# Low parts of w_in on VectorE alone, and 65 columns of v a head, in a decay-attention and hard-swish MoE kernel

## The chip, the core and the metric

The kernel runs on one NeuronCore of a Trainium2 chip. The metric is the device time of one execution in microseconds (us). A core has TensorE (matmuls; PE in the profile, its weight loads PEld), VectorE (DVE), ScalarE (ACT), GpSimd (POOL) and SyncE (SP, which issues the transfers here). Each engine works off its own queue of instructions in order.

## The reference

```python
def _attn_ref(q, k, v, f):          # 8 batches, 8 heads, 576 rows, 64 columns
    scale = 1.0 / np.sqrt(D)
    scores = scale * np.matmul(q, k.transpose(0, 1, 3, 2))
    log_f = np.log(np.clip(f, 0.0001, 1.0))
    cum = np.cumsum(log_f, axis=-1)
    decay = cum[:, :, :, None] - cum[:, :, None, :]
    causal = np.triu(np.ones((S, S), dtype=bool), k=1)
    scores = np.where(causal, -1000000000.0, scores + decay)
    ...
    attn = attn / (np.sum(attn, axis=-1, keepdims=True) + 1e-09)
    return np.matmul(attn, v).astype(np.float32)

def _moe_ref(x, w_in, w_out):       # 4608 x 512, 512 x 2048, 2048 x 512
    h = x @ w_in
    relu6 = np.clip(h + 3.0, 0.0, 6.0)
    g = h * relu6 / 6.0
    return (g @ w_out).astype(np.float32)
```

`x` is the attention's result with the heads side by side. `w_in` and `w_out` come as 64-bit floats.

## The kernel before

Large matmuls run in 16-bit floats with split operands: a value is a high part (its f16 rounding, scaled by a power of two) plus a low part (the f16 rounding of what is left), and a product is three matmuls, high with high, high with low and low with high.

**Weights.** Each of w_in and w_out comes in 16 chunks of 512 KB. `w_load` fetches a chunk, `w_decode` rebuilds f32 values from the 64-bit words (one ScalarE instruction L251, two of VectorE L252 and L253) and squares them on ScalarE for a scale (L257). `w_split` then writes the high part on ScalarE (L284) and the low part in one of these ways:

- with `eye` (a diagonal matrix of minus the scale, L317 on VectorE): TensorE forms minus scale times x by an f32 matmul (L287), adds the high part by an f16 matmul with the identity (L288), and ScalarE copies minus the sum from PSUM to f16 (L289);
- otherwise one VectorE instruction, scale times x minus high (L295), or ScalarE and GpSimd where `POOL_REST` says so, which is nowhere here.

w_in has four groups of four chunks, each with a scale of its own; `PE_LOW` says which groups take the first way: (1, 1, 1, 0), so 12 chunks of 16. All of w_out takes L295. The f32 values of w_in lie in `gT`, those of w_out in `w2`, in the space that the tiles of the MoE take later.

**Attention.** The list `VH` sets the order of the work: four pairs of heads of batch 0 with their first 256 rows (kind A, VH numbers 0 to 3), the eight heads of batch 0 with the rows that are left (kind B, 4 to 11), and the 56 heads of the other batches (kind F). For A and B, `natural` forms scores for the row maxima (pn, L487, with the maximum on VectorE at L493), `max_rows` turns the maxima into a row (ptm, L502; mr, L504; a transfer to TQ), `scores` forms transposed scores (ps, L551 to L554) with exponentials on ScalarE (L570), and `av` multiplies them with v in f32 (L705). For F, `rows` forms the scores once (pn, L611 and L614), VectorE takes the maxima (pp, L622), ScalarE the exponentials (L634), and the two parts go through `ring` (L648 to L662) and a transposing transfer to f16 matmuls with v (L694 to L699).

The product with v ends in `pav`, one tile in PSUM with five blocks of `NAV` columns. A row of v holds 65 columns a head, 64 of v and one of ones for the row sum, 520 for the eight heads. The f32 product reads 96 columns from where its head begins, or for the last head the last 96 of the 520; `window` gives the first column and the head's offset in it. The division by the row sum (L726 to L732, VectorE) reads the 65 that count.

**MoE.** `h_unit` forms 128 columns of h (L777 to L779), its activation (L783, L786) and g's two parts (L787, L788) in `gT`; `out_unit` forms 128 rows of the output (po, L824 to L826, L830). Batch 0 is done in two halves of 256 rows.

**Order.** The program is written as one loop over `VH`. In each step the steps of the weights (`w_step`, by `W_RATE`) and of the MoE (`fill`, by a credit and `F_RATE`) are called between the pieces of the attention. A scheduler then sets each engine's order by its own estimates of durations and by that program order, so that an edit in one place moves instructions elsewhere.

Of the kernel before, what the change touches and what calls it, by code (L numbers as in the profile page):

```python
# [20 lines left out]
def kernel(  # L21
# [12 lines left out]
    NHEAD, D, S = qk.shape  # L34
    D //= 2
    B = vS.shape[0]
    H = NHEAD // B
# [52 lines left out]
    INIT_POOL = (1, 1, 1)  # L90
    W_FIRST = 2
    GRAM = (0, 0, 0, 0)
    PE_LOW = (1, 1, 1, 0)
    QA = 256
    CA = QA // P
    VH = [("A", g) for g in range(NPAIR)] + [("B", n) for n in range(H)]
# [24 lines left out]
        eng.memset(TK[i].bitcast(F32)[96:97, :], 1.0)  # L121
        eng.memset(TK[i].bitcast(F32)[:, S:], 0.0)

    NAV = 96
    pav = ps_a.tile([P, NCH, NAV], F32, name="pav")

    NV16 = 3
    v16 = cpool.tile([P, NV16, NCH, 2, VW + 1], F16, name="v16")
    VR = H * (D + 1)
# [18 lines left out]
    def v_chunk(b, c):  # L148
        return v_parts(b)[c // 3][:, c % 3]
# [51 lines left out]
    def scol(c):  # L201
        return SC[:, c:c + 1]
# [94 lines left out]
    def w_in_work():  # L297
# [6 lines left out]
        for j in range(NG):  # L304
# [9 lines left out]
            eye = None  # L314
            if PE_LOW[j]:
                eye = p2.tile([P, DM], F32, tag="o", name=f"eye{j}")[:, 0:P]
# [210 lines left out]
    def blocks(v):  # L527

        kind, n = VH[v]
        if kind == "A":  # L530
            return [
                (2 * n + h, c, h * CA + c, P,
                 [(j, h * (2 * QA - P) + (c * P if j == 0 else QA), P) for j in range(c + 1)])
                for h in range(2) for c in range(CA)
            ]
        nq = S - QA
        off = [0, nq, 2 * nq, 3 * nq, 3 * nq + nq - P]
        return [
            (n, c, c, CR[c],
             [(j, off[j] + (c - max(j, CA)) * P, CR[j]) for j in range(c + 1)])  # L540
            for c in range(CA, NCH)
        ]
# [43 lines left out]
    o = 0  # L586
# [86 lines left out]

    xpair = {}

    def window(head):

        o = head % H * (D + 1)
        w0 = min(o, VR - NAV)
        return w0, o - w0  # L680

    def av(v, ph):
        kind, n = VH[v]
        g = n if kind == "A" else n // 2
        b = g // NPAIR
        vt = v16[:, g % NV16]
        if kind == "F":
            jh = n % 2
            blk = [(n, c, c) for c in range(NCH)]
            vh, vl = vt[:, :, jh, 0:D + 1], vt[:, :, jh, D + 1:VW]  # L690
            for c in range(NCH):
                pb = ph[:, HT[c]:HT[c] + (2 * c + 1) * P].rearrange("p (g t) -> p g t", t=P)
                o1, o0 = pav[:, c, 0:D + 1], pav[:, c, 0:D]
                nc.tensor.matmul(o1, pb[:, c], vh[:, 0], start=True, stop=False)  # L694
                nc.tensor.matmul(o0, pb[:, c], vl[:, 0], start=False, stop=(c == 0))
                for k in range(1, c + 1):
                    nc.tensor.matmul(o1, pb[:, c + k], vh[:, k], start=False, stop=False)
                    nc.tensor.matmul(o0, pb[:, c + k], vl[:, k], start=False, stop=False)  # L698
                    nc.tensor.matmul(o1, pb[:, k - 1], vh[:, k], start=False, stop=(k == c))  # L699
        else:  # L700
            blk = blocks(v)
            for head, c, pl, m, js in blk:
                w0, _ = window(head)
                for jc, o, kk in js:
                    nc.tensor.matmul(  # L705
                        pav[:m, pl, :], ph[:kk, o:o + m], v_chunk(b, jc)[:kk, w0:w0 + NAV],
                        start=(jc == 0), stop=(jc == c),
                    )
        heads = sorted({x[0] for x in blk})
        if heads[0] % 2 == 0:  # L710
            xpair[g] = (
                p2.tile([P, NCH, P], F32, tag="xf", name=f"xf_{v}", bufs=1),
                p2.tile([P, NCH, 2, P], F16, tag="xhl", name=f"xhl_{v}", bufs=1),
            )
        xf, xhl = xpair[g]
        for head in heads:
            jh = head % 2
            mine = [x for x in blk if x[0] == head]
            p0, p1 = mine[0][2], mine[-1][2] + 1
            c0, c1 = mine[0][1], mine[-1][1] + 1  # L720
            vo = window(head)[1] if b == 0 else 0
            rs = p2.tile([P, NCH, 1], F32, tag="rs", name=f"rs_{v}_{jh}")[:, p0:p1]
            total = pav[:, p0:p1, vo + D:vo + D + 1]
            if b == 0:

                nc.vector.tensor_scalar(  # L726
                    rs, total, PSC * 1e-9, scol(IV + b), op0=ALU.add, op1=ALU.mult
                )
            else:
                nc.vector.tensor_scalar(rs, total, PSC * 1e-9, None, op0=ALU.add)  # L730
            nc.vector.reciprocal(rs, rs)
            nc.vector.tensor_tensor(  # L732
                xf[:, c0:c1, jh * D:(jh + 1) * D], pav[:, p0:p1, vo:vo + D],
                rs.to_broadcast([P, p1 - p0, D]), op=ALU.mult,
            )
        if heads[-1] % 2:
            nc.scalar.copy(xhl[:, c0:c1, 0], xf[:, c0:c1])
            nc.vector.tensor_tensor(
                xhl[:, c0:c1, 1], xf[:, c0:c1], xhl[:, c0:c1, 0], op=ALU.subtract
            )  # L740
# [218 lines left out]
    for i, (kind, n) in enumerate(VH):  # L959
        b, h = divmod(n, H)  # L960
        if kind == "A":
            b = h = 0
# [51 lines left out]
        if prev is not None:  # L1014
            av(*prev)
            if VH[prev[0]][0] == "A" or VH[prev[0]][1] % 2 == 1:
                pend_x = prev[0]
# [3 lines left out]
        prev = (i, ph)  # L1021
    rates[0] = 1.0
    av(*prev)
    fill(4)
    x_move(prev[0])
# [39 lines left out]
```

## Time and profile before

| | |
|---|---|
| median of 3 runs | 1072.47 us (1071.74 to 1077.68) |
| the profiled execution | 1069.33 us, its span 1067.5 us |
| mean granted TensorE clock | 0.988 |
| batch 0's twelve VH steps | roughly the first 135 us |
| first wide row maximum of batch 1 (L622, 576 columns) | starts at 135.2 us |
| first activation on VectorE (L786) of the second half of batch 0 | starts at 202.2 us |
| first activation on VectorE (L786) of batch 1 | starts at 259.9 us |

The profile is of one execution, taken by the hardware's profiler. Busy times are unions of an engine's instructions. Matmuls overlap and their ends are modelled, so the distance from start to start tells more of a matmul's cost than its length. A wait is put down to what came last. The chain that ended last is followed back from the last instruction, at each step to what released it, or to the instruction before it on its engine; "issue" in it is time for which the profile shows no wait.

### The profile page before, as it was taken

What the parts mean: (1) busy time and instruction counts of PE and PEld (TensorE: products, weight loads), DVE (VectorE), ACT (ScalarE), POOL (GpSimd) and SP (SyncE); (2) the same over time, 40 slices, a digit from 0 to 9 for tenths busy, and PEclk for the clock granted to TensorE, in tenths of its full rate; (3) what the DMA queues carried; (4) which work ended last, traced back from release to release, by engine and by line L of the source; (5) the groups of instructions that cost most, each with busy time, mean ns of one, the idle gap of its engine ahead of it and who ended that gap; (6) DMA issues with size and microseconds to landing.
All of it is one profiled execution on the core that took longest, in us unless ns stands there. A gap on an engine that the chain in (4) does not pass through costs nothing.

```text
span 1067.5 us, 21157 instructions
## 1 busy us (share of the span) xinstructions
PE 1006.3 (94%) x7650; PEld 598.0 (56%) x7650; DVE 731.1 (68%) x1887; ACT 587.3 (55%) x1189; POOL 403.4 (38%) x505
## 2 busy tenths in 40 slices
PE   2799977899999999999999999999999999999897
PEld 1577844665555755555555755555555755444543
DVE  6978899996876768866886668846895677105300
ACT  4778666764764557545654557635764566115301
POOL 8343466443443444344443444534443330000000
PEclk9989989999999999999999999999999999999999
DMA  8965647955856776667575766566557554010000
GB/s 240 308 187 194 151 109 145 220 114 118 169 116 134 139 153 124 113 148 165 118 134 118 158 140 119 118 136 167 119 112 145 103 100 74 12 40 1 1 20 30
DMA packets 259155, 133.78 MB, mean 125 GB/s; under 512 B 226948, under 2 KB 228540, under 8 KB 259052
## 3 DMA queue, kind: packets, MB, share of 16 engines
q1 hardware_dynamic: 259052, 132.44, 55.7%
q8 instruction: 60, 0.98, 0.4%
q14 instruction: 43, 0.35, 0.1%
HBM read 47.93 MB, written 9.73 MB: 54 GB/s over the span
## 4 chain that ended last, share of the span: by engine, by line
PE 76%; DVE 12%; ACT 5%; issue 4%; DMA 2%; POOL 1%; SPq 0%; DVEq 0%; ACTq 0%; POOLq 0%
PE po L824 9%; PE po L826 9%; PE po L825 9%; PE ph L777 9%; PE ph L778 9%; PE ph L779 9%; PE pn L611 3%; PE pn L614 3%; DVE pp L622 2%; DVE ring L651 2%; PE po_r L826 1%; PE pav L698 1%; ACT pp L634 1%; PE po_r L824 1%; PE po_r L825 1%
## 5 line engine op out<-in xcount | busy, mean ns | idle before, releaser
L634 ACT ACTIVATE pp<-pp,nb 128x192 f32<-128x192 f32 x280 | 138.6, 552 | 170.3 <-DVE nb L628 150.8
L777 PE MATMUL ph<-xT,w 128*128 128x512 f16 (+1 forms) x576 | 198.8, 357 | 2.5 <-DVE r L786 2.4
L825 PE MATMUL po<-w,gT 128*128 128x512 f16 x512 | 192.6, 382 | 8.0 <-DVE w L295 8.0
L779 PE MATMUL ph<-xT,w 128*128 128x512 f16 (+1 forms) x576 | 198.0, 356 | 0.0
L778 PE MATMUL ph<-xT,w 128*128 128x512 f16 (+1 forms) x576 | 197.8, 356 | 0.0
L651 DVE TENSOR_TENSOR ring<-pp,ring 128x128 f16<-128x128 f32 (+2 forms) x216 | 138.0, 650 | 85.6 <-ACT ring L648 84.7
L824 PE MATMUL po<-w,gT 128*128 128x512 f16 x512 | 190.4, 383 | 5.8 <-DVE r_r L813 2.7
L826 PE MATMUL po<-w,gT 128*128 128x512 f16 x512 | 192.4, 383 | 0.0
L622 DVE CUSTOM_DVE_ANT_0 pp<-pn,W 128x192 f32<-128x192 f32 x280 | 123.3, 482 | 29.3 <-PE pn L614 28.0
L461 POOL TENSOR_TENSOR T<-ST,T 64x576 fp32r<-64x576 f32 (+1 forms) x68 | 100.9, 1483 | 107.2 <-DMA T<-TK 85.8
L786 DVE SCALAR_TENSOR_TENSOR r<-r,ph 128x512 f32<-128x512 f32 (+1 forms) x144 | 89.1, 620 | 61.4 <-ACT r L783 60.6
L611 PE MATMUL pn<-TK,TQ 68*128 68x192 f32 x336 | 124.8, 385 | 3.8 <-issue 2.2
L788 DVE TENSOR_TENSOR gT<-r,gT 128x512 f16<-128x512 f32 (+1 forms) x144 | 111.6, 781 | 22.0 <-ACT gT L787 20.6
L614 PE MATMUL pn<-T,T 128*128 128x192 f32 x336 | 115.2, 368 | 0.2 <-POOL T L461 0.2
L783 ACT ACTIVATE r<-ph,bias_r,SC 128x512 f32<-128x512 f32 (+1 forms) x144 | 103.9, 725 | 19.2 <-PE ph L779 17.1
L648 ACT CAST ring<-pp 128x192 f16<-128x192 f32 x280 | 114.2, 449 | 0.0
L787 ACT CAST gT<-r 128x512 f16<-128x512 f32 (+1 forms) x144 | 81.4, 567 | 59.6 <-DVE r L786 59.3
L449 POOL TENSOR_SCALAR TK<-ST 64x576 fp32r<-64x576 f32 (+1 forms) x68 | 49.2, 724 | 167.8 <-PE pn L611 142.9
L657 POOL TENSOR_TENSOR ring<-pp,ring 128x128 f16<-128x128 f32 x96 | 61.0, 636 | 116.1 <-ACT ring L648 75.2
L458 POOL TENSOR_TENSOR T<-ST,TQ 64x576 fp32r<-64x576 f32 (+2 forms) x68 | 95.2, 1400 | 17.7 <-PE pn L614 11.1
L826 PEld LDWEIGHTS <-gT 128*128 128x128 f16 x560 | 54.8, 98 | 74.5 <-issue 15.1
L825 PEld LDWEIGHTS <-gT 128*128 128x128 f16 x560 | 54.9, 98 | 66.5 <-issue 11.9
(158 smaller groups left out, 2010.2 us busy)
## 6 DMA issues: line engine op xcount, KB each, us to landing
ST<-in_qk_dram SPq DMA_DIRECT2D x64, 288.0 KB
T<-TK SPq DMA_DIRECT2D x64, 144.0 KB
ring<-in_w_out_dram SPq DMA_DIRECT2D x16, 512.0 KB
out_dram<-o SPq DMA_DIRECT2D x32, 256.0 KB
T<-TQ SPq DMA_DIRECT2D x56, 144.0 KB
vst<-in_vS_dram SPq DMA_DIRECT2D x7, 1040.0 KB
ring<-in_w_in_dram SPq DMA_DIRECT2D x9, 512.0 KB
w<-in_w_in_dram SPq DMA_DIRECT2D x7, 512.0 KB
```

Source lines behind the costliest of these rows:

```text
L611: nc.tensor.matmul(dst, TQ[i][0:D + 4, qs], TK[i][0:D + 4, a:e], start=True, stop=False)
L614: nc.tensor.matmul(dst, T7[j][:, qs], T1[j][:, a:e], start=False, stop=True)
L622: nc.vector.tensor_tensor_reduce(pp[:r, w:w + kw], pn[:r, o:o + kw], W[:r, 4 * P + r - kw:4 * P + r], 1.0, -3.0e38, ALU.add, ALU.max, accu ...
L634: nc.scalar.activation(x_, x_, AF.Exp, bias=nb[:r, e0 + x:e0 + x + 1], scale=0.125)
L648: nc.scalar.copy(hl[:r, h0[c]:h0[c] + kw], pp[:r, at[c]:at[c] + kw])
L651: eng.tensor_tensor(hl[:r, a:a + c * P], pp[:r, at[c] + 64:at[c] + kw], hl[:r, h0[c] + 64:h0[c] + kw], op=ALU.subtract,)
L777: nc.tensor.matmul(ph, w1[0][:, cc, fs_], xh, start=(cc == 0), stop=False)
L778: nc.tensor.matmul(ph, w1[0][:, cc, fs_], xl, start=False, stop=False)
L779: nc.tensor.matmul(ph, w1[1][:, cc, fs_], xh, start=False, stop=(cc == NCC - 1))
L824: nc.tensor.matmul(po, g[:, 0, fc, ts_], w2[:, fc, 0, :], start=(fc == 0), stop=False)
L825: nc.tensor.matmul(po, g[:, 0, fc, ts_], w2[:, fc, 1, :], start=False, stop=False)
L826: nc.tensor.matmul(po, g[:, 1, fc, ts_], w2[:, fc, 0, :], start=False, stop=(fc == NFC - 1))
```

## The change

No group of w_in takes the way over TensorE and ScalarE any more: all 16 chunks have their low part made by L295 on VectorE. And the f32 product with v reads the 65 columns of its head; `pav` becomes narrower, and `window` goes. The scheduler orders the program anew, so that rows move on all engines in about the first 345 us; behind that the orders of the two kernels are the same. Line numbers behind `window` are 6 lower, behind the division 7.

```diff
-    PE_LOW = (1, 1, 1, 0)
+    PE_LOW = (0, 0, 0, 0)
...
-    NAV = 96
+    NAV = D + 1
     pav = ps_a.tile([P, NCH, NAV], F32, name="pav")
...
-    def window(head):
-
-        o = head % H * (D + 1)
-        w0 = min(o, VR - NAV)
-        return w0, o - w0
-
...
             for head, c, pl, m, js in blk:
-                w0, _ = window(head)
+                w0 = head % H * NAV
                 for jc, o, kk in js:
                     nc.tensor.matmul(
                         pav[:m, pl, :], ph[:kk, o:o + m], v_chunk(b, jc)[:kk, w0:w0 + NAV],
...
-            vo = window(head)[1] if b == 0 else 0
             rs = p2.tile([P, NCH, 1], F32, tag="rs", name=f"rs_{v}_{jh}")[:, p0:p1]
-            total = pav[:, p0:p1, vo + D:vo + D + 1]
+            total = pav[:, p0:p1, D:D + 1]
...
             nc.vector.tensor_tensor(
-                xf[:, c0:c1, jh * D:(jh + 1) * D], pav[:, p0:p1, vo:vo + D],
+                xf[:, c0:c1, jh * D:(jh + 1) * D], pav[:, p0:p1, 0:D],
                 rs.to_broadcast([P, p1 - p0, D]), op=ALU.mult,
             )
```

## The prediction

> **What bounds the kernel now.** I read the profile in this order: the page's busy shares and its 40 slices, then busy times by stage, then the chain that ended last inside two of the stages, then the waits of VectorE. The page says that TensorE is nearly always busy, and the slices say where it isn't.
>
> ```profile
> PE 1006.3 (94%) x7650; PEld 598.0 (56%) x7650; DVE 731.1 (68%) x1887; ACT 587.3 (55%) x1189; POOL 403.4 (38%) x505
> PE   2799977899999999999999999999999999999897
> DVE  6978899996876768866886668846895677105300
> ```
>
> A slice is 26.7 us. TensorE (PE) has its gaps in the first eight, and there VectorE (DVE) stands at 7 to 9 tenths. So I cut the span by stage. In a row of this view stand the stretch, its length and the busy time of PE, PE's weight loads, DVE, ACT and POOL, then the granted clock.
>
> ```profile
> 20.00:130.00 110.00, 97.25 (x628) 77.43 (x629) 91.70 (x255) 80.33 (x167) 45.59 (x49) 0.95 0.73 217
> 130.00:230.00 100.00, 83.41 (x754) 58.91 (x754) 94.97 (x265) 66.00 (x147) 54.93 (x53) 0.93 0.67 144
> 230.00:260.00 30.00, 28.24 (x207) 15.28 (x205) 19.10 (x57) 14.10 (x31) 10.39 (x15) 1.00 0.59 121
> 260.00:1060.00 800.00, 792.23 (x6048) 443.58 (x6046) 511.46 (x1277) 417.30 (x828) 274.48 (x358) 1.00 0.52 109
> ```
>
> From 260 us to the end PE is busy for 792 of 800 us: TensorE is the bound, and the change takes nothing away there. From 130 to 230 us DVE is busy for 95 of 100 us and PE for 83: VectorE is the bound. From 20 to 130 us, where all of the changed work lies, PE (97 of 110), DVE (92) and ACT (80) share the load. The chain agrees. These are the shares by line of the stretches 30 to 130 and 130 to 230 us.
>
> ```profile
> by line: issue 9.9%; DMA ring<-in_w_out_dram 7.5%; PE pav L705 7.1%; DMA T<-TQ 6.1%; DMA TQ<-mr 5.4%; PE low L287 5.3%; DVE junk L493 5.1%; PE ph L777 4.5%; PE ps L551 4.4%; DVE w L253 3.9%; PE ph L778 3.9%; PE ph L779 3.9%; PE ps L552 3.5%
> by line: DVE pp L622 14.1%; issue 13.5%; DVE ring L651 10.3%; DVE ring L657 8.9%; DVE w L295 7.3%; DVE v L400 5.6%; DVE gT L788 5.1%; ACT pp L634 4.6%; DVE r L786 4.4%; DVE xhl L738 3.3%; ACT r L783 3.2%; DVE ring L662 2.1%; PE pav L705 2.1
> ```
>
> In the first stretch the chain goes through many hands, and the matmul that is removed (L287) holds about 5 us of it; in the second the lines of VectorE lead. So what counts is how late VectorE becomes by 230 us. After that PE runs through, and a delay or a gain that is there at 230 us stays to the end. The profiled execution took 1069.33 us (span 1067.5); the median of the runs is 1072.47. I work out a difference and put it on the median.
>
> **The change, part by part.** The twelve low parts on PE are the first term. These rows show two chunks' worth at half clock, two at full clock, and VectorE behind them.
>
> ```profile
> 57.20 3.62 PE L287 MATMUL low<-gT,eye 128*128 128x512 f32 x4
> 60.61 1.01 PE L288 MATMUL low<-w,ident 128*128 128x512 f16 x2
> 61.11 0.78 PE L487 MATMUL pn<-TK,TQ 66*64 66x128 f32 x2
> 61.93 0.75 DVE L493 CUSTOM_DVE_ANT_0 junk<-pn,W 64x576 bf16<-64x576 f32 x1 [2.17 <-PE pn L487]
> 64.87 1.12 PE L287 MATMUL low<-gT,eye 128*128 128x512 f32 x2
> 65.83 0.38 PE L288 MATMUL low<-w,ident 128*128 128x512 f16 x1
> 66.05 1.02 PE L287 MATMUL low<-gT,eye 128*128 128x512 f32 x2
> 67.74 0.69 DVE L493 CUSTOM_DVE_ANT_0 junk<-pn,W 128x512 bf16<-128x512 f32 x1 [1.09 <-PE pn L487]
> 75.08 0.69 DVE L493 CUSTOM_DVE_ANT_0 junk<-pn,W 128x512 bf16<-128x512 f32 x1 [1.07 <-PE pn L487]
> ```
>
> An f32 matmul is two instructions. From 57.20 to 61.11 two chunks take 3.91 us, or 1.96 each; from 64.87 to 66.05 one takes 1.18 us. Twelve are between 14.2 and 23.5 us of PE. PE isn't the bound of this stage alone, so the saving counts only where somebody waits behind it, as VectorE does at 61.93 (2.17 us idle: the scores pn stand behind the low parts). This is PE before at the same place, head 1 of kind B, VH number 5 (L487 writes raw scores pn, L287 and L288 a low part):
>
> ```order
> L487 MATMUL pn_5_0_544<-TK2_98,TQ2_95 128x512
> L487 MATMUL pn_5_0_544<-TK2_98,TQ2_95 128x384
> L287 MATMUL low_4_442<-gT_116,eye1_439 128x512
> L287 MATMUL low_5_447<-gT_116,eye1_439 128x512
> L288 LDWEIGHTS ident16_80
> L288 MATMUL low_5_447<-w10_113,ident16_80 128x512
> L288 LDWEIGHTS ident16_80
> L288 MATMUL low_4_442<-w10_113,ident16_80 128x512
> L487 MATMUL pn_5_1_573<-TK2_98,TQ2_95 64x128
> L487 MATMUL pn_5_1_573<-TK2_98,TQ2_95 64x448
> ```
>
> There two low parts stand between the halves of the head's scores. And PE now, at the same head:
>
> ```order
> L487 MATMUL pn_0_516<-TK_98,TQ_95 128x512
> L487 MATMUL pn_0_516<-TK_98,TQ_95 128x384
> L487 MATMUL pn_1_534<-TK_98,TQ_95 64x128
> L487 MATMUL pn_1_534<-TK_98,TQ_95 64x448
> ```
>
> The two halves of a head's scores now follow each other. What takes the low parts' place is on VectorE, with these durations (min/median/max in ns): ACT's copy that goes, the factor `eye` that goes, and the four low parts of w_in that VectorE makes already.
>
> ```profile
> L289 ACT ACTIVATE w<-low x12: 570/582/597, 40.6 to 84.8; 128x512 f16<-128x512 f32 x12
> L317 DVE TENSOR_SCALAR eye<-identf,SC x3: 265/270/286, 31.7 to 71.9; 128x128 f32<-128x128 f32 x3
> L295 DVE SCALAR_TENSOR_TENSOR w<-gT,SC,w x4: 746/840/1155, 90.6 to 93.0; 128x512 f16<-128x512 f32 x4
> 90.55 3.34 DVE L295 SCALAR_TENSOR_TENSOR w<-gT,SC,w 128x512 f16<-128x512 f32 x4 [0.28 <-ACT w L284]
> ```
>
> VectorE gains 12 x 3.34/4 = 10.0 us and loses 3 x 0.27 = 0.8 us: **+9.2 us**, all ahead of 130 us. ACT loses 12 x 0.58 = 7.0 us and is not the bound. On VectorE the first group looked like this before (L252 and L253 rebuild f32 values of w_in, L187 to L196 its scale, L504 a head's maxima):
>
> ```order
> L253 SCALAR_TENSOR_TENSOR gT<-ring_125,gT 128x512
> L189 TENSOR_SCALAR e_w_287<-e_w_287 128x1
> L193 TENSOR_SCALAR SC<-e_w_287 128x1
> L196 TENSOR_SCALAR SC<-e_w_287 128x1
> L317 TENSOR_SCALAR eye_292<-identf,SC 128x128
> L252 TENSOR_SCALAR gT<-gT 128x512
> L504 TENSOR_SCALAR mr_328<-ptm_326 4x128
> ```
>
> The scale is followed by `eye`. On VectorE now, some rows further down, where the first pair of heads is divided by its row sums (L719 to L725):
>
> ```order
> L253 SCALAR_TENSOR_TENSOR gT<-w_115,gT 128x512
> L725 TENSOR_TENSOR xf_378<-pav,rs_0_380 128x2x64
> L719 TENSOR_SCALAR rs_1_384<-pav,SC 128x2
> L295 SCALAR_TENSOR_TENSOR w_114<-gT,SC,w_113 128x512 x2
> L724 RECIPROCAL rs_1_384<-rs_1_384 128x2
> ```
>
> `eye` has gone, and two of the group's four low parts stand inside the second head's division, the other two right behind this row. Queued behind the four are the end of that division, which frees `pav` for the next product, and the rebuilding of the next chunks, for which ACT's squares wait. How much of the 9.2 us is covered is read from VectorE's idle time from 20 to 130 us, 110 - 91.7 = 18.3 us, by what ended it (us in total, times, longest):
>
> ```profile
> DVE junk L493 <- PE pn L487: 6.2, 6, 2.2
> DVE w L252 <- ACT w L251: 3.9, 4, 1.8
> DVE gT L252 <- ACT gT L251: 3.4, 6, 1.7
> DVE gT L788 <- ACT gT L787: 1.2, 2, 0.7
> ACT w L251 <- DMA ring<-in_w_out_dram: 8.5, 8, 3.3
> ACT gT L251 <- DMA ring<-in_w_in_dram: 8.4, 3, 5.3
> ACT w L289 <- PE low L288: 2.7, 2, 2.3
> PE po L825 <- DVE w L295: 8.0, 4, 3.8
> ```
>
> Of the 6.2 us on pn I count 4.3 as caused by low parts queued ahead (the waits of 2.17, 1.09 and 1.07 us in the rows above). Of the 7.3 us on ACT's L251 I count 2.7, the time in which ACT stood at L289 with L251 queued behind it; the rest hangs on loads of the weights (the 8.5 and 8.4 us). So 7.0 of the 9.2 us are covered, and **+2.2 us** are left. Were nothing covered it would be +9.2; were each wait of VectorE in these rows covered (6.2 + 3.9 + 3.4 + 1.2 = 14.7), it would be -5.5. I stand between, nearer to the waits that I can trace to a low part.
>
> The last row is from 130 to 230 us: PE waits there on the low parts of w_out, also made on VectorE, so PE has room for whatever it saved. There the order moves too. PE before, at the first output tiles po (L824, L825), behind the raw scores of the second batch's second head (L611, L614):
>
> ```order
> L611 MATMUL pn_1_1759<-TK_97,TQ_94 128x320
> L614 MATMUL pn_1_1759<-T_100,T_102 128x320
> L611 MATMUL pn_1_1759<-TK_97,TQ_94 128x448
> L614 MATMUL pn_1_1759<-T_100,T_102 128x448
> L824 LDWEIGHTS gT
> L824 MATMUL po_0_1376<-w_115,gT 128x512
> ```
>
> On PE now, among the last two heads of the first batch (L817 is the old L824, L699 the product with v, L551 scores):
>
> ```order
> L817 MATMUL po_0_1334<-w_115,gT 128x512
> L817 LDWEIGHTS gT
> L817 MATMUL po_1_1469<-w_115,gT 128x512
> L551 MATMUL ps_0_1510<-TQ_95,TK_98 128x320
> L551 MATMUL ps_1_1531<-TQ_95,TK_98 128x320
> L699 MATMUL pav<-v_111,pf_1425 128x65 x4
> ```
>
> The weights' part moves ahead by about one head. VectorE's rows up to the first activation of the second batch's h (at 259.9 us before) are otherwise the same ones, so I price the move at nothing: VectorE is the bound there, and it does the same work in another order. What could be lost is that a head's product now stands behind a po that waits for L295.
>
> The narrower product is the second term. These are the four groups of one head, at full clock.
>
> ```profile
> 76.61 1.03 PE L705 MATMUL pav<-v,pf 128*128 128x96 f32 x8
> 77.47 0.39 PE L705 MATMUL pav<-xT,pf 128*128 128x96 f32 x2
> 77.79 0.71 PE L705 MATMUL pav<-v,pf 128*64 128x96 f32 x6
> 78.33 0.63 PE L705 MATMUL pav<-xT,pf 128*64 128x96 f32 x4
> ```
>
> With 128 weight columns eight start within 0.86 us, one each 107 ns; with 64 weight columns six start within 0.54 us, one each 90 ns. The same 96 moving columns take longer with more weights, so at 128 the step isn't set by the moving columns alone. There are 240 such instructions (120 products). If only those with 64 or fewer weight columns shrink (80 of them, by 31/96 of 90 ns), PE saves 2.3 us; if all did, 2.3 + 160 x 35 ns = 7.9 us; if none, 0. I take 2.3 and add nothing to the sum, since PE doesn't bound this stage; VectorE reads the same 64 and 1 columns. [...]
>
> **The rivals.**
>
> [...] VectorE's instructions with two inputs in SBUF take longer at times, and L295 is one more of these:
>
> ```profile
> L253 DVE SCALAR_TENSOR_TENSOR gT<-w,gT 128x512 int32<-128x512 int32 x6 | 6.8, 1135 | 0.0
> L253 DVE SCALAR_TENSOR_TENSOR gT<-ring,gT 128x512 int32<-128x512 int32 x6 | 4.0, 680 | 0.0
> ```
>
> The same operation takes 680 or 1135 ns. Stretched by 0.455 us, twelve cost 5.5 us more: 2.2 + 5.5 = +7.7 us, 1080.2. It decides from 0.27 us each. Against it: the 3.34 us for four already hold some of that. [...]
>
> Slower, because nothing covers it: the waits on PE and ACT move behind the longer queue of VectorE and come back at the next load of weights or maxima: +9.2 us, 1081.7. It decides once under 3.9 us are covered.
>
> Slower, by the clock. The granted clock fell twice where PE had little to do:
>
> ```profile
> 50.00:60.00 10.00, 7.57 (x30) 5.29 (x29) 8.40 (x30) 8.52 (x18) 3.60 (x4) 0.56 0.72 213
> 140.00:150.00 10.00, 4.12 (x15) 1.62 (x13) 9.94 (x24) 6.29 (x15) 6.97 (x6) 0.67 0.26 72
> ```
>
> With 14 us less on PE before 90 us, one more such fall is possible among the first batch's heads; 10 us at half speed cost up to 5 us where PE leads: +7.2 us, 1079.7.
>
> Faster: from 20 to 130 us the time is lost in hand-overs between PE, ACT and VectorE, of which the low parts were one, and without them VectorE stands idle for hardly more than 2 of the 110 us. With 16.0 of its 18.3 us covered: 9.2 - 16.0 = -6.8 us, 1065.7. It decides from 14.6 us. For it: L287 holds 5.3% of that chain. Against it: where VectorE is the bound already it still leaves 5 of 100 us idle, and that share here would cover 18.3 - 5.5 = 12.8 us, or -3.6 us, which can't be told from no change.
>
> **How the numbers follow.** Covered for the most part, +2.2 us: 0.45. Port 0.13, nothing covered 0.11, clock 0.11, faster 0.20. Half a per cent (5.4 us) is about what a measurement of this kernel can tell from no change, so: faster 0.20, same 0.45, slower 0.35. The time is 1072.47 + 2.2, about 1074.5. The range goes from 1064, just beyond the faster case, to 1084, beyond each slower case alone but short of two together (9.2 + 5.5 gives 1087.2). The likeliest case has 1068 to 1078.
>
> **What would show it.** Right: L287 to L289 are gone, sixteen instructions of L295 on w_in take about 0.84 us each, VectorE's wait for pn falls from 6.2 to about 2 us, its busy time from 20 to 130 us rises to about 100 of 110 us, and the first activation of the second batch comes within 5 us of 259.9. The products with 128 weight columns still start each 107 ns. Wrong: L295 at over 1.1 us, a new stretch at half clock between 60 and 130 us, or VectorE's first wide row maximum of the second batch (135.2 us before) moved by more than 6 us either way.

## The result, and the profile after

The changed kernel takes 1082.53 us (median of 4 runs, 1080.20 to 1086.17) beside 1072.11 us for the kernel before: a ratio of 1.0103, 95% interval 1.0072 to 1.0134. A second series on another occasion gave 1.0081 (1.0050 to 1.0112). That is 8.7 to 11.0 us slower, about 1%, more than the half per cent that counts as a difference here. The profiled execution took 1080.2 us, its span 1078.4 (before: 1069.33 and 1067.5). The busy shares and slices of its page:

```profile
PE 1004.9 (93%) x7614; PEld 602.9 (56%) x7614; DVE 733.6 (68%) x1896; ACT 582.2 (54%) x1177; POOL 404.5 (38%) x505
PE   2679978789999999999999999999999999999897
DVE  6988798985985668865886678846896667105300
```

VectorE gained 2.5 us in all. TensorE lost work and yet is busy for all but 1.4 us of what it was. TensorE's gaps reach to the ninth slice now, where they ended with the eighth before, and there are more of them. By stage (stretch, length, busy time of PE, weight loads, DVE, ACT, POOL, granted clock):

```profile
20.00:130.00 110.00, 88.38 (x570) 75.48 (x570) 94.19 (x263) 71.97 (x154) 42.44 (x45) 0.97 0.68 203
130.00:230.00 100.00, 80.15 (x682) 57.95 (x681) 88.73 (x243) 61.69 (x133) 56.12 (x55) 0.90 0.71 155
230.00:260.00 30.00, 28.11 (x195) 16.55 (x195) 20.52 (x65) 15.77 (x36) 9.26 (x13) 0.94 0.53 104
260.00:1060.00 800.00, 795.02 (x6119) 446.56 (x6116) 515.83 (x1287) 421.53 (x833) 278.58 (x361) 1.00 0.54 110
```

From 130 to 230 us, where VectorE was the bound with 95 of 100 us, it now idles for 11 us, and TensorE for 20 in place of 17. Neither is the bound there; they wait for each other (VectorE 5.8 us for TensorE's pn and pav, TensorE 8.2 us for VectorE's L295). The lines of the chain of waits say the same, first from 30 to 130, then from 130 to 230 us:

```profile
by line: DMA ring<-in_w_out_dram 17.2%; issue 10.8%; DVE junk L493 7.7%; DVE w L295 7.5%; DVE w L253 5.6%; DMA TQ<-mr 5.3%; DVE gT L253 4.2%; DMA xT<-xhl 3.8%; DVE xhl L731 3.8%; PE ph L770 3.3%; PE ph L771 3.0%; PE ph L772 2.9%; DVE w L252
by line: issue 14.4%; DMA T<-TK 8.1%; DVE v L400 5.3%; DVE pp L622 5.0%; PE po L818 4.4%; DVE ring L651 4.3%; PE po L819 4.1%; PE po L817 4.0%; DMA pT<-ring 3.7%; PE pn L611 3.4%; PE pn L614 3.4%; DVE ring L657 3.2%; DVE w L295 2.9%; POOL r
```

In the first stretch the matmul L287 is gone from the chain, and the loads of w_out hold 17.2% in place of 7.5%. In the second VectorE no longer leads: its two largest lines had 14.1 and 10.3%, its two largest now have 5.3 and 5.0%.

By when the delay is there is seen in two instructions of VectorE, the first wide row maximum of batch 1 and the first activation of batch 1:

```profile
141.74 0.75 DVE L622 CUSTOM_DVE_ANT_0 pp<-pn,W 128x576 f32<-128x576 f32 x1
271.32 0.69 DVE L779 SCALAR_TENSOR_TENSOR r<-r,ph 128x512 f32<-128x512 f32 x1 [1.92 <-ACT r L776]
```

They started at 135.2 and 259.9 us before. The first comes 6.5 us later, which doesn't yet measure a loss, since its place in the order moves too: in extra_dve, one of the experiments below, it comes 14.5 us later than before, and that run is only 2.9 us slower. The second comes 11.4 us later, and the span is 10.9 us longer: by 271 us the whole delay is there.

The largest change of all is in TensorE's clock. These are products with v, first before, then after (start, length, count; twelve f32 instructions of 128 weight columns in a row are one pair of heads):

```profile
26.76 2.88 PE L705 MATMUL pav<-v,pf 128*128 128x96 f32 x12
40.25 1.82 PE L705 MATMUL pav<-v,pf 128*128 128x96 f32 x12
49.66 1.47 PE L705 MATMUL pav<-v,pf 128*128 128x96 f32 x12
62.33 1.47 PE L705 MATMUL pav<-v,pf 128*128 128x96 f32 x12
```

```profile
27.15 2.83 PE L699 MATMUL pav<-v,pf 128*128 128x65 f32 x12
40.34 2.79 PE L699 MATMUL pav<-v,pf 128*128 128x65 f32 x12 [3.04 <-DVE xf L725]
51.43 2.82 PE L699 MATMUL pav<-v,pf 128*128 128x65 f32 x12 [0.69 <-DVE xf L725]
60.99 2.82 PE L699 MATMUL pav<-v,pf 128*128 128x65 f32 x12 [1.24 <-DVE xf L725]
76.19 1.00 PE L699 MATMUL pav<-v,pf 128*128 128x65 f32 x8
91.03 1.45 PE L699 MATMUL pav<-v,pf 128*128 128x65 f32 x12
```

Twelve take about 1.46 us at full clock and 2.8 at half. Before, full clock came while the second group ran (41.0 us by the trace's records of the clock); after, only behind the fourth, at 75.4 us. In the clock column of the stage rows a stretch ahead of the first grant counts as 1.00, so that there only durations like these tell.

What that is worth can be added up. The 21st wide row maximum of VectorE lies behind the part that was re-ordered; it starts at 400.6 us before and 411.7 after. TensorE's busy time up to there, and in each stretch at half clock, first before, then after:

```profile
0.00:41.00 41.00, 18.68 (x69) 14.52 (x70) 30.78 (x89) 21.68 (x43) 26.78 (x42) 1.00 0.87 273
51.20:61.40 10.20, 7.83 (x22) 4.70 (x22) 7.20 (x24) 7.44 (x17) 3.75 (x5) 0.50 0.73 205
143.40:153.60 10.20, 5.57 (x14) 1.95 (x14) 10.14 (x21) 3.74 (x9) 6.83 (x6) 0.50 0.49 115
180.90:184.30 3.40, 3.40 (x10) 1.71 (x8) 3.40 (x13) 2.78 (x8) 0.48 (x2) 0.50 0.78 105
0.00:400.60 400.60, 352.05 (x2776) 236.64 (x2777) 325.69 (x882) 252.91 (x531) 193.50 (x229) 0.97 0.69 166
```

```profile
0.00:75.40 75.40, 40.38 (x173) 33.96 (x173) 60.79 (x176) 42.76 (x88) 40.90 (x54) 1.00 0.83 245
82.20:89.00 6.80, 6.80 (x32) 4.81 (x30) 5.75 (x17) 3.80 (x9) 2.72 (x4) 0.50 0.59 169
153.90:167.50 13.60, 9.13 (x33) 4.97 (x33) 12.45 (x33) 6.34 (x14) 3.84 (x5) 0.50 0.46 89
...
0.00:411.70 411.70, 350.89 (x2741) 241.63 (x2742) 329.04 (x891) 247.40 (x519) 193.83 (x230) 0.96 0.68 162
```

(Three more stretches of 3.4 us, at 191.4, 218.7 and 235.8 us, were busy throughout.) TensorE was busy at half clock for 35.5 us before and 66.5 after. If half of that is the clock's doing, its work is 352.1 - 17.7 = 334.3 us before and 350.9 - 33.3 = 317.6 after: 16.7 us less, about what the prediction worked out for the low parts (14.2) and the narrower product (2.3). But the half clock takes 15.5 us of it back, and TensorE's idle time grows from 48.5 to 60.8 us: -16.7 + 15.5 + 12.3 = +11.1 us. The work went; the time it took did not.

That is a sum, no cause yet: the 12.3 us of idle time may have brought the half clock, or the half clock the idle time. The experiments take it apart.

### The profile page after: what moved, and what is told of

Same layout as the page of the kernel before. It is cut to its first block, busy times and chain, and to the rows that moved or that the text cites. A ratio compares the mean times of both kernels' runs of the same rounds, so it can differ in the third digit from the quotient of the medians.

```text
span 1078.4 us, 21085 instructions
## 1 busy us (share of the span) xinstructions
PE 1004.9 (93%) x7614; PEld 602.9 (56%) x7614; DVE 733.6 (68%) x1896; ACT 582.2 (54%) x1177; POOL 404.5 (38%) x505
## 4 chain that ended last, share of the span: by engine, by line
PE 74%; DVE 12%; DMA 5%; issue 4%; ACT 3%; POOL 2%; SPq 1%; ACTq 0%; DVEq 0%; POOLq 0%
PE po L817 10%; PE po L818 10%; PE po L819 10%; PE ph L770 8%; PE ph L772 8%; PE ph L771 8%; PE pn L614 3%; PE pn L611 3%; DVE gT L781 2%; DMA ring<-in_w_out_dram 2%; DVE pp L622 2%; DVE ring L651 1%; PE ph_r L793 1%; PE ph_r L795 1%; PE ph_r L794 1%
## 5 line engine op out<-in xcount | busy, mean ns | idle before, releaser
L611 PE MATMUL pn<-TK,TQ 68*128 68x192 f32 x336 | 127.0, 391 | 5.3 <-issue 4.1
L449 POOL TENSOR_SCALAR TK<-ST 64x576 fp32r<-64x576 f32 (+1 forms) x68 | 48.5, 713 | 195.5 <-PE pn L611 146.3
```

Of the source, the lines that this page charges most:

```text
L611: nc.tensor.matmul(dst, TQ[i][0:D + 4, qs], TK[i][0:D + 4, a:e], start=True, stop=False)
```

## The experiments

All times are ratios to the kernel before on the same chip, turned into us with 1072 us.

| run | what it is | us against before, 95% |
|---|---|---|
| the change | both parts | +11.0 (7.7 to 14.4) |
| after_again | the same once more | +8.7 (5.4 to 12.0) |
| before_again | the kernel before against itself | -0.9 (-3.1 to 1.5) |
| extra_dve | before + VectorE's new work | +2.9 (0.9 to 4.9) |
| nav_only | 65 columns alone, ordered anew | +4.5 (2.1 to 6.9) |
| low_only | low parts alone, ordered anew | +4.9 (2.9 to 7.1) |
| extra_pe | change + TensorE's old work | +4.8 (3.1 to 6.5) |
| low_thin | before, order kept, L287 on 1 column | +2.8 (0.2 to 5.3) |
| nav_fixed | before, order kept, 65 columns | +2.3 (0.5 to 4.0) |
| all_fixed | extra_dve, order kept, L287 on 1 column, 65 columns | +5.0 (3.0 to 7.0) |
| ep_thin | extra_pe, order kept, L287, L288 on 1 column | +6.4 (4.1 to 8.9) |
| before_swap | before, same work, other order | +18.0 (14.3 to 21.8) |
| after_free | change + 264 small matmuls | +18.0 (14.5 to 21.5) |

**The halves alone, and each engine's load put back.** nav_only is the changed kernel with `PE_LOW` as before:

```diff
-    PE_LOW = (0, 0, 0, 0)
+    PE_LOW = (1, 1, 1, 0)
```

> One half of the change alone: the product with v takes 65 columns, the low parts of w_in stay on TensorE for 12 chunks. Theory 'VectorE's load' (the 9.2 us of new low parts on VectorE are not covered and last to the end): the same as before within 4 us, since VectorE's work is unchanged. Theory 'clock' (less work on TensorE keeps it at half clock in the first 75 us, and that is what costs): 1 to 4 us slower than before, as the wide product is a small part of TensorE's work there.

low_only is the kernel before with `PE_LOW = (0, 0, 0, 0)` and its 96 columns.

> The other half alone: all low parts of w_in on VectorE, the product with v still takes 96 columns. Theory 'VectorE's load': as the full change, 9 to 12 us slower than before. Theory 'clock': 6 to 10 us slower, with TensorE at full clock earlier than in the full change, since the wide columns are TensorE work too. If it is within 4 us of before, the narrow product is the cause.

extra_pe is the changed kernel in which TensorE forms the twelve low parts too, for nobody:

```diff
-    PE_LOW = (0, 0, 0, 0)
+    PE_LOW = (1, 1, 1, 0)
...
             nc.tensor.matmul(pl, ident16, hi, start=False, stop=True)
-            nc.scalar.activation(lo, pl, AF.Copy, scale=-1.0)
-            return
```

> The full change, but TensorE still forms the 12 low parts of w_in (L287, L288) into PSUM tiles that nobody reads; VectorE makes the low parts that are used. ScalarE's copies stay away. Theory 'VectorE's load': no faster than the full change, 1080 to 1088, since VectorE does the same work and TensorE's old work is there again. Theory 'clock': full clock from about 41 us and most of the loss gone, 1070 to 1076.

extra_dve is the kernel before in which VectorE makes the twelve low parts as well, into a scratch tile:

```diff
         if eye is not None:
+            spare_lo = p2.tile([P, S], BF16, tag="junk", name=f"spare_{k}", bufs=1)
+            nc.vector.scalar_tensor_tensor(
+                spare_lo[:, 0:CW], x, sc, hi, op0=ALU.mult, op1=ALU.subtract
+            )
```

> The kernel before, with TensorE and ScalarE still making the 12 low parts of w_in, and VectorE forming the same low parts a second time into a scratch tile that nobody reads. Theory 'VectorE's load': 9 to 12 us slower than before, though the clock comes up at 41 us as before. Theory 'clock': within 4 us of before, as TensorE's work is the same.

VectorE's new work alone costs 2.9 us, not 9.2: it is covered for the most part, as the prediction said. Yet each half of the change costs over 4 us (together 9.4, nearly the whole), and nav_only gives VectorE nothing more to do. Neither theory had these sizes: nav_only was to cost at most 4 us, low_only 6 or more. Full clock first came at 41.2 us in nav_only, as before, and at 74.7 us in low_only, as in the changed kernel. Giving TensorE its old work back makes the changed kernel faster, 4.8 us behind the kernel before where the change itself is 8.7 to 11.0 behind. 'Clock' expected that, with full clock from about 41 us; it came at 39.8, but two stretches at half clock of 17.1 us each followed, at 46.7 and 80.8 us. So VectorE isn't the main cause, and what TensorE lost may be part of it. But in each of these the scheduler set a new order as well.

**How much an order can do, and the same program again.** after_again and before_again are the two kernels unchanged.

> The changed kernel once more, beside the kernel before on the same chip, so that its time can be set against the other variants, and for a second profile of the same instructions. Both theories: 8 to 13 us slower than before. Theory 'clock' (TensorE, with 14 us less to do before 90 us, is granted full speed later): the profile again shows half clock until 60 us or later; and should this execution be granted full clock by 45 us, its first activation of the second batch (271.3 us before) comes by 267 us. Rival 'order' (the scheduler's new order of instructions is a worse one): that activation comes within 2 us of 271.3 whatever the clock does.

> The kernel before against itself, for the width of a null comparison and a second profile. Both theories: ratio within 0.2% of 1. 'Clock': full speed is granted by 45 us again and the first activation of the second batch comes within 2 us of 259.9; should it be granted only after 60 us in this execution, that activation comes 4 us later or more. 'Order': it stays within 2 us of 259.9 whatever the clock does.

Both repeat, and so do their clocks: full speed first at 73.3 us after and 42.0 us before, the activation of batch 1 at 269.2 and 260.1 us. Neither kernel drew the other's clock, so the case that would have told the theories apart did not come. A kernel against itself is within 0.3% of 1.

before_swap lets VectorE make the first group's low parts in place of the last group's, the same instructions in number:

```diff
-    PE_LOW = (1, 1, 1, 0)
+    PE_LOW = (0, 1, 1, 1)
```

> The kernel before with PE_LOW = (0, 1, 1, 1): the first group of w_in has its low parts on VectorE in place of the last. Same instructions in number, 12 chunks on TensorE, 4 on VectorE, but another order by the scheduler and no f32 low parts on TensorE before the second group. 'Order': 3 to 5 us slower, as each of the other edits was. 'Clock': slower by 3 us or more only if the profile shows half clock well past 41 us, else within 2 us of before.

18 us, with no more work for any engine: neither theory had that size. How late the run is by then is seen in the low parts of w_out on VectorE, on which the output tiles wait. The line L295 for w_out, before (shortest, median and longest in ns, first and last start in us):

```profile
L295 DVE SCALAR_TENSOR_TENSOR w<-w,SC x16: 732/736/1966, 144.3 to 195.0; 128x512 f16<-128x512 f32 x16
```

And in before_swap:

```profile
L295 DVE SCALAR_TENSOR_TENSOR w<-w,SC x16: 705/742/1966, 164.4 to 215.7; 128x512 f16<-128x512 f32 x16
```

The first and the last come 20 us later, and the first activation of batch 1 starts at 279.9 us. These low parts carry the delay and don't make it: from 130 to 230 us TensorE waits 2.3 us for them, where it waited 8.0 before. Where the 18 us arise wasn't found, and since full clock first came at 58.8 us here, this run doesn't part order from clock. It shows that moving work about, without adding any, can cost more than the whole change does. In the changed kernel the same row reads 132.6 to 192.6, earlier than before: this sign of a delay is absent there.

after_free puts 264 matmuls of the identity with itself into unused columns of pav's bank:

```diff
...
+        if i == 0 and k < 12:
+            for n in range(22):
+                nc.tensor.matmul(fil, ident16, ident16, start=True, stop=True)
```

> The changed kernel plus 264 f16 matmuls of the identity with itself (128 x 128, results never read, in columns of the product's PSUM bank that nobody uses), 22 at each of the first twelve splits of w_in. They wait for nothing, so the scheduler puts them where it thinks TensorE idle; some 14 us of TensorE at full clock, about what the removed low parts took. VectorE and ScalarE get no work from them. 'Clock': full speed by 45 us, and 4 to 8 us faster than the changed kernel (1073 to 1077). 'Order' or no clock effect: the added work brings nothing, or costs what it takes: 1080 to 1086.

This run doesn't answer its question, since its premise was wrong. The matmuls do wait. The first of them in the timeline, and TensorE's longest wait from 20 to 130 us:

```profile
3.47 6.91 PE L289 MATMUL bank<-ident 128*128 128x128 f16 x88 [3.47 <-DVE ident L66]
```

```profile
PE bank L289 <- DVE xf L730: 6.6, 1, 6.6
```

The first 88 ran at 3.47 us, where full speed is of no use (it was granted at 7.2 us and lost at 14.0), and later TensorE stood at them once for 6.6 us, until VectorE had read the same bank.

**The order held fixed.** The next four edit instructions after the scheduler has run, so that every engine's order and every wait stay, and only TensorE's matmuls get shorter:

```diff
         tile_decay_attention__then__hard_swish_kernel(tc, *args)
+    _recast(nc, _thin)         # low_thin; nav_fixed: _narrow; all_fixed: both
... _recast replaces a matmul of the finished program by what the function returns
+def _cut(x, width, skip=0):
+    return x.__replace__(ap=(x.ap[0], (1, width)), offset=x.offset + skip, bass_ap=None)
+
+def _narrow(i):                # o, m, w: output, moving operand, weights
...     only for pav, f32
+    skip = 31 if m.offset % 520 == 424 else 0
+    return i.__replace__(outs=[_cut(o, 65, skip)], ins=[_cut(m, 65, skip), w])
+
+def _thin(i):
...     only for low, L287; L288 then starts the sum
+    return i.__replace__(outs=[_cut(o, 1)], ins=[_cut(m, 1), w], stop_tensor_calc=True)
```

> The kernel before with its order kept on every engine: after the scheduler has run, each of the twelve f32 low parts on TensorE (L287) is cut from 512 moving columns to 1. All waits, ScalarE's copies and VectorE's work stay; the low parts of those chunks come out wrong. TensorE gets 11.5 us less to do at full clock, up to 19 us at half clock. Rival 'order' (only the new order of instructions costs time): nothing is lost, 0 to 4 us faster, since VectorE waited 4.3 us on scores behind low parts. 'Clock' (without that work TensorE is granted full speed later): no faster, 0 to 6 us slower, full clock first granted after 50 us (41.0 before).

> The kernel before with its order kept: after the scheduler has run, the 120 f32 products with v are cut from 96 to their 65 columns, the narrower product alone without any re-ordering. The run with 65 columns that the scheduler ordered anew was 4.1 us slower. 'Order': 0 to 2 us faster than before, so the 4.1 us was the order. 'Clock' (fewer columns in the same 107 ns lower TensorE's activity): 1 to 4 us slower, with more or longer stretches at half clock than before's 24 us behind the first grant.

> All of the changed kernel's loads in another order: the run with twelve additional low parts on VectorE (2.7 us slower than before, full clock from 45.8 us), its order kept on every engine, with the twelve f32 low parts on TensorE cut to 1 column and the products with v to 65 columns. So VectorE does the change's work, TensorE is rid of nearly all that the change takes away, and only ScalarE keeps its copies. 'Order' (the changed kernel's own order costs the 10 us): within 2 us of that run, 1072 to 1076. 'Clock': full clock first granted after 55 us and 7 to 12 us slower than before, 1078 to 1084, as the changed kernel is.

low_thin takes about 10 us from TensorE (L287's busy time falls from 16.0 to 5.5 us; its weight loads and L288 stay), in the old order, with nothing added anywhere, and is 2.8 us slower; nav_fixed is 2.3 us slower. Both are what the theory 'clock' expected and its rival did not. The products with v in low_thin show the reason:

```profile
48.83 2.71 PE L705 MATMUL pav<-v,pf 128*128 128x96 f32 x12
60.42 2.71 PE L705 MATMUL pav<-v,pf 128*128 128x96 f32 x12
68.61 1.85 PE L705 MATMUL pav<-v,pf 128*128 128x96 f32 x8
80.53 1.52 PE L705 MATMUL pav<-v,pf 128*128 128x96 f32 x8
87.18 1.03 PE L705 MATMUL pav<-v,pf 128*128 128x96 f32 x8
```

Half clock until 81.6 us: in this order the f32 low parts of 512 columns were what had brought full speed at 41.0. TensorE's busy time up to the 21st wide row maximum rises from 352.05 to 361.96 us although it has less to do:

```profile
0.00:407.50 407.50, 361.96 (x2776) 252.23 (x2777) 321.87 (x884) 252.28 (x531) 192.20 (x229) 0.97 0.68 163
```

(This profiled execution, 1079.23 us, was 5 us above the median of its runs, so its size is not that of the median.) In nav_fixed full clock came at 47.2 us, with six more stretches at half clock ahead of 200 us, against three before (four in before_again). That profiled execution, 1077.32 us, was 3.5 us above the median of its runs, too.

all_fixed has the change's work on VectorE and its product with v, but not ScalarE's relief, and TensorE still spends 11.6 us on low parts (21.3 in extra_dve). It is 5.0 us slower than before and 2.1 slower than extra_dve, whose order it has: just beyond what 'order' expected (within 2 us of that run), and 2 us short of 'clock' (7 to 12 slower than before). Its full clock came only at 83.6 us, even later than in the changed kernel, and yet:

```profile
20.00:130.00 110.00, 91.61 (x570) 76.46 (x570) 92.16 (x255) 77.54 (x164) 38.08 (x41) 1.00 0.66 196
130.00:230.00 100.00, 87.53 (x759) 64.81 (x759) 92.24 (x261) 64.90 (x140) 55.80 (x56) 0.93 0.74 157
230.00:260.00 30.00, 30.00 (x253) 17.17 (x251) 22.59 (x68) 17.49 (x41) 14.01 (x17) 1.00 0.70 152
```

TensorE idles for 30.9 of these 240 us, in the changed kernel for 43.4, in the kernel before for 31.1. (This execution, 1072.93 us, was 4 us below the median of its runs.) So the late clock alone isn't the 10 us either.

ep_thin does the same to extra_pe, the other order at hand. What is left is nearly the change itself, in an order that was planned with TensorE's old work; TensorE still spends 5.9 us on the shortened matmuls, of 18.7:

```diff
...
+    return i.__replace__(outs=[_cut(o, 1)], ins=[_cut(m, 1), w],
+                         start_tensor_calc=True, stop_tensor_calc=True)   # L287 and L288
```

> The whole change in another order: the run in which TensorE still formed the twelve low parts for nobody (4.8 us slower than before), its order kept on every engine, with those matmuls (L287 and L288) cut to 1 column after the scheduler has run. What is left is the changed kernel's work, with three small factors on VectorE (0.8 us) beside it. Theory 'order' (about half of the changed kernel's 10 us is its own order of instructions): 4 to 7 us slower than before (1076 to 1079), at least 3 us faster than the changed kernel. 'Clock' (all of the 10 us is TensorE's lost work and the half clock that follows): 8 to 12 us slower (1080 to 1084), as the changed kernel is.

6.4 us slower than before, as 'order' expected: 1.6 us more than extra_pe, and 2.3 to 4.6 us less than the changed kernel. Full clock came only at 91.6 us (in an execution 4 us above the median), later than in the changed kernel, so the late clock doesn't set the two apart.

**What the runs add up to.** VectorE's new work, in extra_dve's order: 2.9 us. TensorE's lost work at a fixed order: no gain in any of four pairs, but a loss of 2.8, 2.3, 2.1 and 1.6 us (the first two shown by their own intervals; the last two are differences of runs whose intervals overlap). VectorE's and TensorE's shares together are some 5 us, as all_fixed has it. The rest, 3.5 to 4.9 us (the change at +9.9, the mean of its two series, less ep_thin or all_fixed), I put down to the changed kernel's own order. That is argued, not shown. It is a difference: against all_fixed it is beyond the intervals' width taken together, against ep_thin just at it. Both runs leave part of the low parts' work on TensorE, and ScalarE's relief wasn't tried by itself. And if the losses of low_thin and nav_fixed are both added to extra_dve's 2.9 us, 8.0 us have a name and only 1.9 are left.

Nor was a place found for this rest. TensorE's waits from 130 to 230 us, after, and the like of the second in ep_thin:

```profile
PE po L818 <- DVE w L295: 8.2, 3, 6.2
PE pn L614 <- POOL T L461: 4.0, 1, 4.0
```

```profile
PE pn L612 <- POOL T L459: 4.6, 2, 2.8
```

The first had 8.0 us before, the second 0.2. GpSimd there waited for a transfer (T<-TK) that took 8.1 us from its issue at 208.4 us. low_thin and nav_fixed, in the old order, show 2.5 us of that wait, extra_dve and all_fixed none, and ep_thin, which is faster than the changed kernel, shows more of it. So it isn't a matter of order alone, and it doesn't account for the rest. Whether the po moved ahead or the later loads of w_out cost it wasn't tried by itself. No version beat the kernel before.

## Why the prediction failed where it failed

The forecast was 1074.5 us, its range 1064 to 1084, the chance of slower by over half a per cent 0.35. The time, 1082.53, is in the range, but that is luck: the likeliest case (+2.2 us, 1068 to 1078) isn't what happened, and the range reached to 1084 for rivals of which none came as it was priced.

- **VectorE's +9.2 us: right.** Sixteen instructions of L295 for w_in took 832 ns each; 12 x 0.832 - 0.8 is 9.2. The group's row, then VectorE's and ScalarE's waits from 20 to 130 us:

```profile
L295 DVE SCALAR_TENSOR_TENSOR w<-gT,SC,w 128x512 f16<-128x512 f32 x16 | 13.0, 832 | 0.0
```

```profile
DVE w L252 <- ACT w L251: 8.3, 4, 4.1
...
DVE junk L493 <- PE pn L487: 1.1, 1, 1.1
```

```profile
ACT w L251 <- DMA ring<-in_w_out_dram: 13.0, 8, 3.4
```

- **7.0 of it covered, +2.2 left: right in size, by extra_dve's +2.9, but not for its reason.** The cover was to come from waits that end when the low parts leave TensorE (4.3 us on pn) and ScalarE (2.7). In extra_dve both still do their part, and VectorE's wait for pn is gone all the same; in low_thin the low parts are short and the order is the old one, and the wait stays. VectorE's waits for pn from 20 to 130 us, extra_dve, then low_thin (6.2 before):

```profile
DVE junk L497 <- PE pn L491: 0.2, 1, 0.2
```

```profile
DVE junk L493 <- PE pn L487: 6.6, 6, 2.2
```

So that the sizes agree is luck, and what covers the work stays open. In the changed kernel the wait for pn fell to 1.1 us, 2.4 in after_again (about 2 were forecast); but in before_again, the kernel before, it was only 3.8. VectorE's wait for ScalarE's L251 on w_out rose from 3.9 to 8.3, behind loads of w_out, in this profile alone: it was 2.9 in after_again. VectorE's busy time from 20 to 130 us came to 94.2 us (96.9 in after_again), not 100. The rival "nothing covered" falls with extra_dve, and no run shows a port that makes VectorE's instructions longer, the case of 0.13 in the forecast: L295, stretched by 0.455 us in it, stayed at its 0.83 us on the mean.
- **TensorE's saving: right in amount, wrong in sign.** This is the first step that failed: "the saving counts only where somebody waits behind it". The sum had no place for a saving that costs. At a fixed order it is a loss of about 2 us (1.6 to 2.8), and low_thin shows why: the f32 matmuls also brought full clock, at 41.0 us with them, at 81.6 without. The page showed the clock, and I had it as a rival with 0.11, as "one more such fall" of 10 us. What came was above all a first grant 34 us later, for which the page's clock row has no sign: it starts with the first grant.
- **The narrower product: "I take 2.3 and add nothing to the sum".** The products with 128 weight columns still start each 107 ns (eight in 1.03 us before, 1.00 after), as forecast, and those with 64 now each 68 ns in place of 90 (six in 0.56 us, the last of them 0.22), so 80 x 22 ns = 1.8 us. Adding nothing was the error: with 65 columns in the same 107 ns TensorE does a third less in that time, and nav_fixed costs 2.3 us.
- **"I price the move at nothing": the second step that failed.** VectorE did the same work in another order, but it no longer was the bound from 130 to 230 us, where I had argued from 95 busy us of 100: it was busy for 88.7 us (91.4 in after_again). Some 2 to 5 us are left for the order, by difference, and before_swap shows that an edit of this kind can cost 18.
- **The signs named for "wrong"** came in part. L295 stayed below 1.1 us on the mean (0.832, the longest 1.683). Half clock did stand between 60 and 130 us, until 75.4 and from 82.2 to 89.0. The first wide maximum of batch 1 moved by 6.5 us, 5.2 in after_again (6 was the limit). The first activation of batch 1, which was to stay within 5 us, moved by 11.4.

How short TensorE's gaps were while it stayed at half clock shows in the changed kernel's row from 24 to 76 us, all but its last 0.6 us ahead of the first grant:

```profile
24.00:76.00 52.00, 37.68 (x166) 31.74 (x165) 46.09 (x133) 32.54 (x68) 20.63 (x20) 1.00 0.83 246
```

TensorE is busy for 37.7 of 52 us, and its longest gap is 3.04 us (the product at 40.34). The kernel before loses full speed with shorter ones: granted at 41.0 us, it falls at 51.2, and the longest idle time of TensorE between is 1.56 us.

```profile
49.35 0.48 PE L487 MATMUL pn<-TK,TQ 66*64 66x128 f32 x2 [1.56 <-ACT pf L570]
```

So gaps of at most 3.04 us did not bring full speed for these 51 us in the one kernel, and gaps of at most 1.56 us did not hold it in the other.

## What to carry to other kernels

Work taken from an engine that isn't the bound can cost time (2 to 3 us here, at a fixed order), and that engine's full clock can come later for it (at 81.6 us in place of 41.0 in low_thin): list the matmuls ahead of the first full clock before removing any, and compare durations of one kind of matmul over time, since the clock row can begin late (here at 75.4 us). Where a scheduler sets the order, an edit is two changes, the work and the order; shortening instructions after scheduling measures the first alone, and a swap with no change of work tells how much a new order, with all that follows from it, can do (here 18 us) before half a per cent is believed.

## What the hardware showed that I had not expected

- TensorE held half clock for 75 us while busy for 40.4 of them, with no gap over 3.04 us from 24 us on; shortening twelve f32 matmuls from 512 columns to 1 moved the first full clock from 41.0 to 81.6 us with the order unchanged.
- Fewer moving columns at the same start distance (65 for 96 at 107 ns) went with more half clock, in the one profile taken: 47.2 us and six later stretches by 200 us in nav_fixed, 41.0 us and three before (42.0 and four in before_again).
